# Loading a kernel's input into the upper half of its residual block, in one order with the weights

## The chip, the cores and the metric

The kernel runs on one core of one Trainium2 chip. The time is that of the device for one execution, in microseconds. An execution of a kernel on one core repeats to within 0.2%. A profile is one execution; its span is about 1.8 us shorter than the time.

Engines: PE is TensorE (matmuls, with PEld its weight loads), DVE is VectorE, ACT is ScalarE, POOL is GpSimd, SP is SyncE. L295 is line 295 of the kernel that the profile belongs to.

## The reference, cut to what matters

Four layers on x of 2048 x 1024 in bf16: linear attention (A), gated MLP (B), A, B, each with a layer norm in front and a residual add behind.

```python
def A(x, wqkv, wo):              # 32 heads of 32
    q, k, v = split(x @ wqkv)
    phi = lambda t: where(t > 0, t + 1, exp(t)) + 1e-6
    kv = einsum("bhsd,bhse->bhde", phi(k), v)
    z  = einsum("bhsd->bhd", phi(k))
    return (phi(q) @ kv / (phi(q) @ z + 1e-6)) @ wo
def B(x, Wg, Wu, Wd):
    g = x @ Wg
    return ((g * (g > 0)) * (x @ Wu)) @ Wd

x = x + A(layernorm(x));  x = x + B(layernorm(x))
x = x + A(layernorm(x));  x = x + B(layernorm(x))
```

## The kernel before

x is 16 row blocks of 128 rows, and a quarter is four blocks. For each quarter the attention layer normalises four blocks, transposes them into `xnT`, and runs 16 groups of eight 512-column matmuls: the two halves of the keys (k0, k1), then the two of the values (v0, v1), each for four blocks. Then come the small kv matmuls. When all four quarters are through, the query stage starts. The very first quarter is transposed by PE, all others by DMA transposes.

```python
def ln_norm(self, layer, t):
    src = self.xin.pop(t) if layer == 0 else self.x[t]      # xin: bf16 buffers, 3 of them
    ...bn_stats x2, bn_aggr (DVE); Ln, Exp (ACT) give rstd...
    nc.vector.tensor_scalar(out=xn, in0=src, ...)           # xn: 2 buffers
    if layer == 0:
        nc.gpsimd.tensor_copy(out=self.x[t], in_=src)       # bf16 -> fp32 residual
        if t + 3 < self.ST:
            self.load_x(t + 3)                              # issued on ACT's queue

def phi(self, ps, out):                                     # keys: ACT, then DVE twice
    nc.scalar.activation(out=e, in_=ps, func=ACT.Exp)
    nc.vector.tensor_scalar(out=e, in0=e, ...min, add)
    nc.vector.scalar_tensor_tensor(out=out, in0=ps, ..., in1=e)

# layer A, cut
ring.free_before((l, "k0"))                     # loads 7 weights of 1 MB on SP's queue
for q in range(self.NQ):
    if l == 0 and q == 0:
        for j in range(QT):
            self.ln_turn(l, j, self.ln_norm(l, j))          # PE transposes
    if q + 1 < self.NQ:
        self.ln_later(l, q + 1, 2, 4, 2)                    # norm + DMA transposes of the next quarter
    for c, name in enumerate(("k0", "k1", "v0", "v1")):
        for j in range(QT):
            ...eight matmuls into ps...
            ...keys: self.phi(ps, ...); values: one nc.scalar copy...
            if c == 3:
                later.at(2, lambda t=t: kv_step(t))
            later.tick()
```

## Time and profile before

| what | before |
|---|---|
| time, median of 4 runs | 1679.51 us (1679.11 to 1679.56) |
| first useful 512-column matmul | 14.82 us |
| first query matmul of layer 0 | 141.82 us |
| first gate matmul (layer 1) | 269.00 us |
| key/value stage of layer 2, which has no start-up | 117.58 us |

Read it from the end. PE is busy 98% of the span, so what counts is where PE is not busy or runs slowly. The waits of PE give the places, the timeline gives the moments, and a second pass over the same work (layer 2) gives the yardstick. The prediction below shows those lines.

### The profile page before, as it was taken

How to read it: one execution, taken by the hardware profiler on the slowest of the kernel's cores; microseconds unless marked ns; L12 is line 12 of the kernel's file. 1: busy time of each engine (PE TensorE's matmuls, PEld its weight loads, DVE VectorE, ACT ScalarE, POOL GpSimd, SP SyncE). 2: the span in 40 equal slices, each digit the busy share in tenths (PEclk: the TensorE clock that was granted, in tenths of full speed). 3: DMA queues.
4: the chain of work that ended last, by engine and by line, in shares of the span. 5: the costliest groups of instructions: out<-in, count | busy, mean ns of one | idle time of the engine just before them, and what ended most of it. 6: DMA issues, size and time to landing. Idle time of an engine off the chain costs nothing.

```text
span 1677.8 us, 18805 instructions
## 1 busy us (share of the span) xinstructions
PE 1651.6 (98%) x7824; PEld 752.0 (45%) x7824; DVE 572.4 (34%) x972; ACT 365.3 (22%) x693; POOL 20.9 (1%) x54
## 2 busy tenths in 40 slices
PE   6999999999999999999999999999999999999999
PEld 3444444444444444444444444444444444444444
DVE  6435895213211321321143289932111112211111
ACT  3335641110110111011023374411001101100110
POOL 2100000000000000000000000000000000000000
PEclk9999999999999999999999999999999999999999
DMA  9403133446545544654530222444554464465440
GB/s 270 82 25 121 31 82 94 148 154 184 166 136 163 158 152 158 183 157 136 168 99 1 76 76 38 95 120 141 170 186 152 131 192 136 146 188 165 147 152 28
DMA packets 261847, 218.28 MB, mean 130 GB/s; under 512 B 67201, under 2 KB 259713, under 8 KB 261761
## 3 DMA queue, kind: packets, MB, share of 16 engines
q1 hardware_dynamic: 254848, 208.69, 42.0%
q10 hardware_dynamic: 6912, 8.39, 1.6%
q8 instruction: 61, 1.00, 0.3%
q14 instruction: 26, 0.20, 0.0%
HBM read 197.13 MB, written 4.19 MB: 120 GB/s over the span
## 4 chain that ended last, share of the span: by engine, by line
PE 91%; DVE 5%; ACT 2%; DMA 2%; issue 1%; DVEq 0%; ACTq 0%
PE acc L383 23%; PE pu L366 23%; PE pg L366 23%; PE ps L232 12%; PE ps L301 5%; PE ps L314 3%; DVE stats L130 2%; DMA xin<-in_A_x_dram 1%; DVE xn L137 1%; PE kv L207 1%; PE ps L272 1%; DVE x L318 1%; DVE pq L276 0%; DMA xnT<-xn 0%; ACT r L274 0%
## 5 line engine op out<-in xcount | busy, mean ns | idle before, releaser
L366 PEld LDWEIGHTS <-t 128*128 128x128 bf16 x3584 | 350.7, 98 | 422.9
L366 PE MATMUL pg<-xnT,t 128*128 128x512 bf16 x1792 | 423.3, 379 | 0.0
L366 PE MATMUL pu<-xnT,t 128*128 128x512 bf16 x1792 | 423.3, 379 | 0.0
L383 PE MATMUL acc<-t,hT 128*128 128x512 bf16 x1792 | 388.1, 379 | 0.0
L372 DVE TENSOR_TENSOR hT<-pu,rg 128x512 bf16<-128x512 f32 x224 | 154.9, 692 | 591.5 <-PE pu L366 591.5
L371 ACT ACTIVATE rg<-pg 128x512 f32<-128x512 f32 x224 | 133.6, 597 | 764.9 <-PE pg L366 764.9
L383 PEld LDWEIGHTS <-hT 128*128 128x128 bf16 x1792 | 175.3, 98 | 211.4
L232 PE MATMUL ps<-t,xnT 128*128 128x512 bf16 x1024 | 229.1, 382 | 0.4 <-DVE pkv L179 0.4
L232 PEld LDWEIGHTS <-xnT 128*128 128x128 bf16 x1024 | 99.5, 98 | 115.5 <-issue 3.3
L301 PE MATMUL ps<-xnT,t 128*128 128x512 bf16 x512 | 121.3, 379 | 0.2
L314 PE MATMUL ps<-T,pq 128*128 128x512 bf16 x512 | 112.8, 379 | 0.0
L177 ACT ACTIVATE e<-ps 128x512 f32<-128x512 f32 x128 | 76.0, 594 | 82.0 <-PE ps L232 65.1
L178 DVE TENSOR_SCALAR e<-e 128x512 f32<-128x512 f32 x128 | 55.0, 430 | 112.0 <-ACT e L177 111.3
L134 ACT ACTIVATE rstd<-mv,eps 128x1 f32<-128x1 f32 x64 | 18.8, 295 | 321.0 <-DVE mv L132 320.8
L394 DVE TENSOR_TENSOR xo<-x,acc 128x512 bf16<-128x512 f32 x32 | 22.0, 688 | 171.1 <-PE acc L383 169.8
L314 PEld LDWEIGHTS <-pq 128*128 128x128 bf16 x512 | 50.1, 98 | 59.0
L301 PEld LDWEIGHTS <-t 128*128 128x128 bf16 x512 | 49.8, 98 | 55.5 <-issue 1.0
L391 DVE TENSOR_TENSOR x<-x,acc 128x512 f32<-128x512 f32 x32 | 21.6, 676 | 149.5 <-PE acc L383 148.4
L130 DVE BATCH_NORM_STATS2 stats<-x 128x6 f32<-128x512 f32 x96 | 66.2, 690 | 2.0
L238 ACT ACTIVATE pkv<-ps 128x512 bf16<-128x512 f32 x64 | 38.3, 598 | 75.2 <-PE ps L232 70.2
L276 DVE TENSOR_TENSOR pq<-pq,r 128x512 bf16<-128x512 bf16 x64 | 43.8, 689 | 7.9 <-ACT r L275 5.3
L274 ACT ACTIVATE r<-ps,eps 128x512 f32<-128x512 f32 x64 | 43.4, 686 | 9.0 <-PE ps L272 8.3
(41 smaller groups left out, 410.5 us busy)
## 6 DMA issues: line engine op xcount, KB each, us to landing
t<-in_B_W_gate_dram SPq DMA_DIRECT2D x56, 1024.0 KB, 6.0
t<-in_B_W_up_dram SPq DMA_DIRECT2D x56, 1024.0 KB, 5.3
t<-in_B_W_down_dram SPq DMA_DIRECT2D x64, 896.0 KB, 6.0
t<-in_A_wqkv_dram SPq DMA_DIRECT2D x12, 1024.0 KB, 6.6
xin<-in_A_x_dram ACTq DMA_DIRECT2D x16, 256.0 KB, 4.4
t<-in_A_wo_dram SPq DMA_DIRECT2D x4, 1024.0 KB, 5.2
out_dram<-xo ACTq DMA_DIRECT2D x32, 128.0 KB, 2.3
xnT<-xn SPq DMA_TRANSPOSE x60, 3.1
```

The lines of the kernel that those rows point to most:

```text
L130: nc.vector.bn_stats(out=stats[:, c, :], in_=src[:, c * fmax:(c + 1) * fmax])
L177: nc.scalar.activation(out=e, in_=ps, func=ACT.Exp)
L178: nc.vector.tensor_scalar(out=e, in0=e, scalar1=1.0, scalar2=1e-6, op0=ALU.min, op1=ALU.add)
L232: nc.tensor.matmul(ps, lhsT=self.xnT[l, q][:, kt, j * P:(j + 1) * P], rhs=w[:, kt, :], start=(kt == 0), stop=(kt == KT - 1))
L274: nc.scalar.activation(out=r, in_=ps, func=ACT.Ln, bias=self.eps6[:, 0:1])
L276: nc.vector.tensor_tensor(out=p, in0=p, in1=r, op=ALU.mult)
L301: nc.tensor.matmul(ps, lhsT=w[:, kt, (g % 4) * P:(g % 4 + 1) * P], rhs=self.xnT[l, sc][:, kt, :], start=(kt == 0), stop=(kt == KT - 1))
L314: nc.tensor.matmul(ps, lhsT=pq[sc, g // 4][:, g % 4, j * P:(j + 1) * P], rhs=T[g // 2][:, g % 2, n2 * NW:(n2 + 1) * NW], start=(g == 0), s ...
L366: nc.tensor.matmul(ps, lhsT=w[:, kt, fi * P:(fi + 1) * P], rhs=self.xnT[l, q][:, kt, :], start=(kt == 0), stop=(kt == KT - 1))
L371: nc.scalar.activation(out=rg, in_=pg, func=ACT.Relu)
L372: nc.vector.tensor_tensor(out=h[:, fi, :], in0=pu, in1=rg, op=ALU.mult)
L383: nc.tensor.matmul(acc[j], lhsT=hT[ft // 4][:, ft % 4, j * P:(j + 1) * P], rhs=wd[:, k, :], start=(ft == 0), stop=(ft == self.FT - 1))
```

## The change

The intent is to start PE sooner:

- x goes by DMA, as bf16, straight into the upper half of its own fp32 residual block. The cast on GpSimd and the three-buffer limit go away, and the residual add of layer 0 reads the bf16.
- All loads go out on SP's queue in one order: block 0 in halves, half of the first weight, block 1, and so on.
- Values ahead of keys, and the first eight groups in pairs of blocks, so that blocks 2 and 3 are wanted later.
- The transposes of each of the first four blocks in two halves; the identity made directly in bf16.
- Ten idle matmuls at the outset, for the clock.

```diff
+        self.xb = [x[:, D // 2:D].bitcast(BF16) for x in self.x]
-        src = self.xin.pop(t) if layer == 0 else self.x[t]
+        src = self.xb[t] if layer == 0 else self.x[t]
-        if layer == 0:
-            nc.gpsimd.tensor_copy(out=self.x[t], in_=src)
-            if t + 3 < self.ST:
-                self.load_x(t + 3)
-        self.nc.scalar.dma_start(out=xin, in_=self.x_v[:, t, :])
+        self.nc.sync.dma_start(out=self.xb[t][:, lo:hi], in_=self.x_v[:, t, lo:hi])
...
+    def head(self):
+        zero = self.ep.tile([P, NW], BF16, tag="e")
+        nc.vector.memset(zero, 0.0)
+        idle = self.ps3.tile([P, NW], F32, tag="b")
+        for _ in range(10):
+            nc.tensor.matmul(idle, lhsT=zero[:, 0:P], rhs=zero, start=True, stop=True)
+        self.load_x(0, 0)
+        self.load_x(0, 1)
+        ring.load_part(H)          # first half of v0
+        self.load_x(1)
+        ring.load_to(2)            # rest of v0, v1
+        self.load_x(2)
+        self.load_x(3)
+        ring.load_to(3)            # k0
+        ...blocks 4 to 7, k1, blocks 8 to 15, the other three weights...
...
-        for n in ("k0", "k1", "v0", "v1", "o0", "q0", "q1", "o1"):
+        for n in ("v0", "v1", "k0", "k1", "o0", "q0", "q1", "o1"):
...
+                order = [(c, j + i) for i in (0, 2) for c in range(2) for j in range(2)] + order[8:]
-                        later.at(2, lambda t=t: kv_step(t))
+                    later.at(3, lambda t=t: kv_step(t))
...
-        ident_f = self.xnp.tile([P, P], F32, tag="xn")
-        make_identity(nc, ident_f[:, :])
-        nc.vector.tensor_copy(out=self.ident, in_=ident_f)
+        make_identity(nc, self.ident[:, :])
```

More of the change, by code (lines that the diff above doesn't have):

```diff
@@ L23, in __init__, with load_part @@
         self.nc, self.pool, self.depth = nc, pool, depth
-        self.plan, self.tiles, self.loaded = [], {}, 0
+        self.plan, self.tiles, self.loaded, self.part = [], {}, 0, 0
     def add(self, name, src):
         self.plan.append((name, src))
+    def load_part(self, k):
+        name, src = self.plan[self.loaded]
+        t = self.pool.tile([P, 8, NW], BF16, tag="w")
+        self.nc.sync.dma_start(out=t[:, 0:k, :], in_=src[:, 0:k, :])
+        self.tiles[name], self.part = t, k
     def load_to(self, n):
@@ L31, in load_to @@
             name, src = self.plan[self.loaded]
-            t = self.pool.tile([P, 8, NW], BF16, tag="w")
-            self.nc.sync.dma_start(out=t[:, 0:src.shape[1], :], in_=src)
-            self.tiles[name] = t
+            if self.part == 0:
+                t = self.pool.tile([P, 8, NW], BF16, tag="w")
+                self.tiles[name] = t
+            k, m = self.part, src.shape[1]
+            self.nc.sync.dma_start(out=self.tiles[name][:, k:m, :], in_=src[:, k:m, :])
+            self.part = 0
             self.loaded += 1
@@ L93, in __init__ @@
         self.ep = pool("ep", 3)
-        self.xio = pool("xio", 3)
+        self.xo = pool("xo", 3)
         self.xnp = pool("xnp", 2)
@@ L102, in __init__ @@
         self.later = _Later()
-        self.n_evac = 0
-        ident_f = self.xnp.tile([P, P], F32, tag="xn")
         from concourse.masks import make_identity
-        make_identity(nc, ident_f[:, :])
         self.ident = self.const.tile([P, P], BF16, name="ident")
-        nc.vector.tensor_copy(out=self.ident, in_=ident_f)
+        make_identity(nc, self.ident[:, :])
         self.mask = self.const.tile([P, P], F32, name="mask")
@@ L118, in __init__, with ln_stat, ln_rstd @@
         self.x = [self.xres.tile([P, D], F32, name=f"x{t}") for t in range(self.ST)]
-        self.xin = {}
+        self.xb = [x[:, D // 2:D].bitcast(BF16) for x in self.x]
         self.xnT = {}
-    def ln_norm(self, layer, t):
-        nc, D = self.nc, self.D
-        src = self.xin.pop(t) if layer == 0 else self.x[t]
-        fmax = min(nc.vector.BN_STATS_FMAX, D)
-        nch = D // fmax
-        stats = self.small.tile([P, nch, nc.vector.BN_STATS_DIM], F32, tag="stats")
-        for c in range(nch):
-            nc.vector.bn_stats(out=stats[:, c, :], in_=src[:, c * fmax:(c + 1) * fmax])
+    def ln_stat(self, t, src, c, stats):
+        fmax = self.D // 2
+        self.nc.vector.bn_stats(out=stats[:, c, :], in_=src[:, c * fmax:(c + 1) * fmax])
+    def ln_rstd(self, stats):
+        nc = self.nc
         mv = self.small.tile([P, nc.vector.BN_AGGR_DIM], F32, tag="mv")
@@ L135, in ln_norm, with ln_scale @@
         nc.scalar.activation(out=rstd, in_=rstd, func=ACT.Exp, scale=-0.5)
-        xn = self.xnp.tile([P, D], BF16, tag="xn")
-        nc.vector.tensor_scalar(out=xn, in0=src, scalar1=mv[:, 0:1], scalar2=rstd[:, 0:1],
-                                op0=ALU.subtract, op1=ALU.mult)
-        if layer == 0:
-            nc.gpsimd.tensor_copy(out=self.x[t], in_=src)
-            if t + 3 < self.ST:
-                self.load_x(t + 3)
-        return xn
+        return mv, rstd
+    def ln_scale(self, src, mv, rstd, xn=None, h=None):
+        if xn is None:
+            xn = self.xnp.tile([P, self.D], BF16, tag="xn")
+        w = self.D // 2
+        s = slice(None) if h is None else slice(h * w, (h + 1) * w)
+        self.nc.vector.tensor_scalar(out=xn[:, s], in0=src[:, s], scalar1=mv[:, 0:1],
+                                     scalar2=rstd[:, 0:1], op0=ALU.subtract, op1=ALU.mult)
+        return xn
@@ new lines, in ln_norm, with turn @@
+    def ln_norm(self, layer, t):
+        nc = self.nc
+        src = self.xb[t] if layer == 0 else self.x[t]
+        stats = self.small.tile([P, 2, nc.vector.BN_STATS_DIM], F32, tag="stats")
+        for c in range(2):
+            self.ln_stat(t, src, c, stats)
+        xn = self.ln_scale(src, *self.ln_rstd(stats))
+        return xn
+    def head(self):
+        nc, tc, ring = self.nc, self.tc, self.ring
+        H = self.KT // 2
+        zero = self.ep.tile([P, NW], BF16, tag="e")
[11 more added lines that the diff above has]
+        ring.load_to(3)
+        self.load_x(4)
+        self.load_x(5)
+        self.load_x(6)
+        self.load_x(7)
+        ring.load_to(4)
+        for t in range(8, self.ST):
+            self.load_x(t)
+        ring.load_to(7)
+        src = self.xb
+        self.xnT[0, 0] = self.xnTp.tile([P, self.KT, QT * P], BF16, tag="xnT", name="xnT0_0")
+        stats = [self.small.tile([P, 2, nc.vector.BN_STATS_DIM], F32, tag="stats", name=f"st{j}")
+                 for j in range(QT)]
+        def turn(j, xn, h):
+            tp = self.ps3.tile([P, H, P], BF16, tag="b")
+            for i in range(H):
+                kt = h * H + i
+                nc.tensor.transpose(tp[:, i, :], xn[:, kt * P:(kt + 1) * P], self.ident)
+            dst = self.xnT[0, 0][:, h * H:(h + 1) * H, j * P:(j + 1) * P]
+            if h == 0:
+                nc.vector.tensor_copy(out=dst, in_=tp)
+            else:
+                nc.scalar.activation(out=dst, in_=tp, func=ACT.Copy)
+        with tc.manual_schedule(engines={mybir.EngineType.DVE, mybir.EngineType.Activation}):
+            for j in range(QT):
+                for c in range(2):
+                    self.ln_stat(j, src[j], c, stats[j])
+                r = self.ln_rstd(stats[j])
+                xn = self.xnp.tile([P, self.D], BF16, tag="xn")
+                for h in range(2):
+                    if j == 0 or h == 0:
+                        self.ln_scale(src[j], *r, xn, h if j == 0 else None)
+                    turn(j, xn, h)
@@ L150, in ln_turn @@
                                                 name=f"xnT{layer}_{q}")
-        dst = self.xnT[layer, q][:, :, j * P:(j + 1) * P]
-        if layer or q:
-            nc.sync.dma_start_transpose(out=dst, in_=xn)
-            return
-        tp = self.pst.tile([P, self.KT, P], BF16, tag="tr")
-        for kt in range(self.KT):
-            nc.tensor.transpose(tp[:, kt, :], xn[:, kt * P:(kt + 1) * P], self.ident)
-        self.n_evac += 1
-        if self.n_evac % 2:
-            nc.vector.tensor_copy(out=dst, in_=tp)
-        else:
-            nc.scalar.activation(out=dst, in_=tp, func=ACT.Copy)
+        nc.sync.dma_start_transpose(out=self.xnT[layer, q][:, :, j * P:(j + 1) * P], in_=xn)
     def ln_later(self, layer, q, first, step, lag):
@@ L180, in phi, with load_x @@
                                        op0=ALU.max, op1=ALU.add)
-    def load_x(self, t):
-        xin = self.xio.tile([P, self.D], BF16, tag="xio")
-        self.nc.scalar.dma_start(out=xin, in_=self.x_v[:, t, :])
-        self.xin[t] = xin
+    def load_x(self, t, c=None):
+        D = self.D
+        lo, hi = (0, D) if c is None else (c * D // 2, (c + 1) * D // 2)
+        self.nc.sync.dma_start(out=self.xb[t][:, lo:hi], in_=self.x_v[:, t, lo:hi])
     def plan_A(self, l):
@@ L200, in layer_A @@
         ring, later = self.ring, self.later
-        kv = [self.ps3.tile([P, NW], F32, tag="b", name=f"kv{l}_{i}") for i in range(3)]
         pk, va = {}, {}
@@ L212, in kv_step @@
             del pk[t], va[t]
-        ring.free_before((l, "k0"))
+        if l == 0:
+            self.head()
+        else:
+            ring.free_before((l, "v0"))
+        kv = [self.ps3.tile([P, NW], F32, tag="b", name=f"kv{l}_{i}") for i in range(3)]
         for q in range(self.NQ):
+            if q + 1 < self.NQ:
+                self.ln_later(l, q + 1, 4 if l == 0 and q == 0 else 2, 3 if l == 0 and q == 0 else 4, 2)
+            order = [(c, j) for c in range(4) for j in range(QT)]
             if l == 0 and q == 0:
-                for j in range(QT):
-                    self.ln_turn(l, j, self.ln_norm(l, j))
-            if q + 1 < self.NQ:
-                self.ln_later(l, q + 1, 2, 4, 2)
-            for c, name in enumerate(("k0", "k1", "v0", "v1")):
-                w = ring.get((l, name))
-                for j in range(QT):
-                    t = q * QT + j
-                    if c == 0:
-                        s = self.slab.tile([P, 2 * D + G], BF16, tag="slab", name=f"pkv{l}_{t}")
-                        pk[t] = s[:, 0:D]
-                        va[t] = s[:, D:2 * D + G].rearrange("p (g e) -> p g e", e=P + 1)
-                        nc.gpsimd.memset(va[t][:, :, P:P + 1], 1.0)
-                    ps = self.ps.tile([P, NW], F32, tag="a")
-                    for kt in range(KT):
-                        nc.tensor.matmul(ps, lhsT=self.xnT[l, q][:, kt, j * P:(j + 1) * P],
-                                         rhs=w[:, kt, :], start=(kt == 0), stop=(kt == KT - 1))
-                    if c < 2:
-                        self.phi(ps, pk[t][:, c * NW:(c + 1) * NW])
-                    else:
-                        g0 = (c - 2) * (NW // P)
-                        nc.scalar.activation(
-                            out=va[t][:, g0:g0 + NW // P, 0:P],
-                            in_=ps[:, :].rearrange("p (g e) -> p g e", e=P), func=ACT.Copy)
-                    if c == 3:
-                        later.at(2, lambda t=t: kv_step(t))
-                    later.tick()
@@ new lines, in layer_A @@
+                order = [(c, j + i) for i in (0, 2) for c in range(2) for j in range(2)] + order[8:]
+            for c, j in order:
+                w = ring.get((l, ("v0", "v1", "k0", "k1")[c]))
+                t = q * QT + j
+                if c == 0:
+                    s = self.slab.tile([P, 2 * D + G], BF16, tag="slab", name=f"pkv{l}_{t}")
+                    pk[t] = s[:, 0:D]
+                    va[t] = s[:, D:2 * D + G].rearrange("p (g e) -> p g e", e=P + 1)
+                    nc.gpsimd.memset(va[t][:, :, P:P + 1], 1.0)
+                ps = self.ps.tile([P, NW], F32, tag="a")
+                for kt in range(KT):
+                    nc.tensor.matmul(ps, lhsT=self.xnT[l, q][:, kt, j * P:(j + 1) * P],
+                                     rhs=w[:, kt, :], start=(kt == 0), stop=(kt == KT - 1))
+                if c >= 2:
+                    self.phi(ps, pk[t][:, (c - 2) * NW:(c - 1) * NW])
+                else:
+                    g0 = c * (NW // P)
+                    nc.scalar.activation(
+                        out=va[t][:, g0:g0 + NW // P, 0:P],
+                        in_=ps[:, :].rearrange("p (g e) -> p g e", e=P), func=ACT.Copy)
+                if c == 3:
+                    later.at(3, lambda t=t: kv_step(t))
+                later.tick()
@@ L316, in out_units @@
                                          start=(g == 0), stop=(g == G - 1))
-                    xs = self.x[t][:, n2 * NW:(n2 + 1) * NW]
-                    nc.vector.tensor_tensor(out=xs, in0=xs, in1=ps, op=ALU.add)
+                    cols = slice(n2 * NW, (n2 + 1) * NW)
+                    xs = self.x[t][:, cols]
+                    nc.vector.tensor_tensor(out=xs, in0=self.xb[t][:, cols] if l == 0 else xs,
+                                            in1=ps, op=ALU.add)
                     later.tick()
         ring.free_before((l, "o0"))
-        later.at(3, finish_kv)
-        q_units(0, 4)
+        later.at(4, finish_kv)
+        q_units(0, 5)
         fold_wo()
@@ L392, in layer_B @@
                         else:
-                            xo = self.xio.tile([P, NW], BF16, tag="xio")
+                            xo = self.xo.tile([P, NW], BF16, tag="xo")
                             nc.vector.tensor_tensor(out=xo, in0=xs, in1=acc[j], op=ALU.add)
@@ L402, in run @@
         nc.scalar.preload_act_table_set("natural_log_exp_and_others")
-        for t in range(3):
-            self.load_x(t)
         self.layer_A(0, 1)
```

## The prediction

> **What bounds the kernel now.** The page first: it says which engine sets the time.
>
> ```profile
> span 1677.8 us, 18805 instructions
> PE 1651.6 (98%) x7824; PEld 752.0 (45%) x7824; DVE 572.4 (34%) x972; ACT 365.3 (22%) x693; POOL 20.9 (1%) x54
> ```
>
> TensorE (PE) is busy for all but 26.2 us, so no change that leaves the matmuls alone can win more than that plus what cold-clock matmuls waste. Next, the waits of PE over the whole span (engine, tile, line, awaited instruction: total us, times, longest):
>
> ```profile
> PE tp L157 <- DVE ident L109: 12.2, 1, 12.2
> PE ps L272 <- DVE pq L179: 3.5, 6, 0.8
> PE tp L157 <- DVE xnT L160: 2.7, 2, 1.9
> PE kv L207 <- ACT pkv L238: 2.6, 1, 2.6
> ```
>
> Three of these four, 17.5 us, lie in the first 47 us of layer 0. The PE rows of the timeline there (start, us, line, operation, count, idle time before):
>
> ```profile
> 12.22 1.01 PE L157 MATMUL tp<-ident,xn 128*128 128x128 bf16 x8 [12.22 <-DVE ident L109]
> 14.02 1.01 PE L157 MATMUL tp<-ident,xn 128*128 128x128 bf16 x8 [0.78 <-DVE xnT L160]
> 14.82 2.76 PE L232 MATMUL ps<-t,xnT 128*128 128x512 bf16 x6
> 21.21 0.61 PE L157 MATMUL tp<-ident,xn 128*128 128x128 bf16 x8 [1.88 <-DVE xnT L160]
> 46.93 0.40 PE L207 MATMUL kv<-pkv 128*128 128x129 bf16 x4 [2.63 <-ACT pkv L238]
> ```
>
> The first useful 512-column matmul starts at 14.82, and six of them take 2.76 us (0.46 each). Layer 2 does the same work with no start-up, so I use it as the yardstick. Its key/value stage runs from 849.16 to 966.74 (first and last row below); layer 0's ends where line L301 takes over, at 141.82.
>
> ```profile
> 849.16 24.34 PE L232 MATMUL ps<-t,xnT 128*128 128x512 bf16 x112
> 966.74 1.89 PE L301 MATMUL ps<-xnT,t 128*128 128x512 bf16 x8
> 141.82 1.89 PE L301 MATMUL ps<-xnT,t 128*128 128x512 bf16 x8
> ```
>
> Layer 2: 117.58 us for 512 matmuls (0.216 us each, from 1.73 us per 8) plus the small kv ones. Layer 0: 141.82. **The whole start-up costs 24.2 us.** From L301 to the next layer both take about 127.2 us (layer 0's first gate matmul is at 269.00), so nothing else distinguishes them.
>
> Last, the chain of waits, for why layer 0 is late, and one row of the one-microsecond windows for the transfers (window, length, PE clock, DMA share, GB/s):
>
> ```profile
> 1.21 7.09 DMA xin<-in_A_x_dram
> 12.90 5.68 DMA xin<-in_A_x_dram
> 24.56 5.75 DMA xin<-in_A_x_dram
> 43.23 3.66 DMA xnT<-xn
> 13.00:14.00 1.00, 1.00 1.09 346
> ```
>
> Row blocks of x wait 5.7 to 7.1 us because three 1 MB weight loads run beside them and only three x buffers exist. The rate is about 250 GB/s from 2 to 4 us and 345 to 389 after: the transfers are saturated, so order decides. The identity's cast, a 0.20 us instruction queued late on DVE, holds the first transpose until 12.2.
>
> **What the Trainium skill says.** "TensorE: Matmul & The Clock Gate", Part 1: the array runs at half clock until busy for about 3.4 us, and falls back after an idle window of that length. The trace agrees: 0.46 us per matmul at 14.82 against 0.216 later, and 8 matmuls take 2.46 us on the chain after the 2.63 us gap at 43-47. "DMA: Bandwidth & Descriptors", section "Issuing engines are not separate DMA queues": issuing from two engines only saves issue time, the transfers interleave. The trace agrees: x loads (ACT queue) land 2.8 to 7.6 us after issue while the weights share the bandwidth. "SBUF — State Buffer", section "SBUF: two separate sides": DVE's two-port operations and GpSimd exclude each other. The trace agrees: normalising a block took 1.05 us beside a GpSimd cast, 0.55 us without.
>
> **The change part by part.** I use the built program's instruction order for the changed kernel and the durations above.
>
> 1. *One load order.* All of x and the seven weights (11.5 MB) go out on one queue. Estimated cumulative landing at 250 then 355 GB/s, plus 0.7 us to be seen: block 0 (two halves) about 3.3 us; half of v0, 5.5; block 1, 6.2; rest of v0, 7.7; v1, 10.7; block 2, 11.4; block 3, 12.1; k0, 15; k1, 21; the last weight about 36. Weights are in time: k0 is wanted near 23, k1 near 30.
>
> 2. *Path to the first matmul.* Two statistics at 0.65 (one already during the load), aggregation 0.19, the two small ScalarE steps 0.29 and 0.20, half a block normalised (about 0.3), with gaps: about 5.4. GpSimd now makes the identity in bf16 by about 2 us, so its wait (12.2) is gone.
>
> 3. *Idle matmuls.* Ten from 1.8 us, after the memset. At 0.43 cold and some warm at the end they finish near 5.9; they may hold the first transposes by half a microsecond, but the clock is then up, which saves about 1.5 us of cold matmuls. Four transposes, a copy: first useful matmul about 6.8 instead of 14.82.
>
> 4. *Pairs, values first.* After the eight matmuls of block 0, PE waits for block 1: its statistics start on DVE near 7.0 (1.3), aggregation, rstd, 0.55 of normalising: transposes at 9.7. Then 11 matmuls to 12.9. Block 2 lands at 11.4; the same DVE chain ends at 14.0, so PE idles about 1.1. Fifteen matmuls to 17.8, block 3 about 0.5 late: 18.3, its eight transposes end at 18.8. By then 34 matmuls (7.3 us) are done: **11.5 us lost** including 32 transposes. Values need only a ScalarE copy where keys need one ScalarE and two DVE steps (0.59, 0.43, 0.67), which leaves DVE to the statistics.
>
> 5. *Next quarter.* 94 matmuls and a kv step follow: the second quarter starts near 39.6. Its DMA transposes are queued behind all 11.5 MB, so the first lands near 38; an issue takes 1.23 us on SP, a landing 3.1 us or more, and only two normalised buffers exist, so the third lands near 42.3 and the fourth near 44. They are wanted at 44.5 and 46.2. DVE waits for these landings ahead of some key work, so a kv step may slip. I charge 0.8 us, against the 2.6 idle plus about 1.7 of cold clock after it today.
>
> 6. *No casts.* Sixteen GpSimd casts (1.04 each) and their wait for x are gone; GpSimd was never on PE's path, the gain is DVE's and already counted. The residual add reads bf16 instead of fp32; its 0.68 us is beside PE.
>
> Sum: loss in layer 0 falls from 24.2 to 11.5 + 0.8, about 12.3; the gain is 11.9. Layers 1 and 3 are unchanged. In layer 2 only the order of values and keys and the lag of kv change: no stall exists there to remove, and I count zero, within 1 us. 1679.5 - 11.9 = **1667.6 us**, 0.7% less.
>
> **Rivals.** *(a) The transpose wait replaces the x wait.* All 11.5 MB now stand ahead of the first DMA transpose. For it: the saturated rate, and the two-buffer chain. Against it: no x load competes with the transposes any more, and PE needs them only near 40. If the rate is 320 instead of 355, they come 3 to 4 us later, PE idles about 3 more and cools: about 1672. *(b) DVE sets the pace of the first four blocks*, not the loads: block 2 at the earliest near 13.3 in place of 14.0. For it: statistics, aggregation and normalising make some 3 us per block against 3.5 us of matmuls for its pair of value groups. The time would be 1666.5 to 1667, so nearly the same. *(c) The early gain is given back later*, because other waits absorb it. Against it: from 55 us on PE is full at the warm clock and the weights of the next stages are loaded ahead (the DMA share falls to 0.00 at 60-80 us), so an earlier start moves everything: no loss. *(d) The reordering hurts layers 0 and 2*: keys last put the long exp/min/max chain just before the kv steps and the end of the stage, where the masked kv is needed. Worth up to 1 or 2 us per layer: about 1670.
>
> **Range and chances.** Doubt is in the landing of block 2 (1 us), the transposes (-0.8 to +4) and the key order (-1 to +3): 1664.5 to 1672. Faster by 2% means below 1646; that is 33 us, more than all the start-up loss of 24.2. Slower by 2% would need 33 us of new stalls, and nothing here comes to that. So same: 0.98.
>
> **What would show it.** PE's first row: ten matmuls from about 1.8 us. First useful matmul at 6 to 8 us at about 0.22 to 0.25 us each; no wait on the identity. PE idle before the transposes of block 1 near 1 us, block 2 near 1, block 3 near 0.5. The first query-stage matmul of layer 0 near 130 instead of 141.8, and layer 2's stage still 117.6 long. Wrong if block 2's transposes start after 16 us, if PE idles over 3 us at 38-50, or if layer 2 gains new waits.

## The result, and the profile after

The changed kernel takes 1667.58 us, median of four runs (1667.28 to 1669.95), against 1679.51 (1679.11 to 1679.56). The ratio is 0.9933, with a 95% interval of 0.9915 to 0.995. That is the mean time of one kernel's runs over that of the other's of the same rounds, so not quite the ratio of the medians. The difference of the medians is 11.9 us, or 0.7%.

The page of the changed kernel:

```profile
span 1665.9 us, 18656 instructions
PE 1644.1 (99%) x7678; PEld 751.3 (45%) x7834; DVE 571.6 (34%) x975; ACT 364.9 (22%) x695; POOL 4.8 (0%) x38
```

The span is 11.9 us shorter. GpSimd's casts are gone (4.8 us busy instead of 20.9), and DVE and ScalarE do the same work as before. PE's sum can't be compared: its 7678 matmul records against 7834 weight loads show that about 150 are missing from this trace.

The waits of PE in the changed kernel over the whole span, without the query-stage ones (engine, tile, line, awaited instruction: total us, times, longest):

```profile
PE idle L171 <- DVE zero L168: 2.0, 1, 2.0
PE tp L198 <- DVE xn L149: 1.8, 2, 1.5
PE ps L295 <- DVE xnT L201: 0.8, 2, 0.5
PE ps L295 <- ACT xnT L203: 0.3, 1, 0.3
```

The wait of 12.2 us is gone, as are those of 2.7 and 2.6. Some 3 us remain in the first 20 us, apart from the two in front of the idle matmuls. PE's timeline of the changed kernel, cut:

```profile
1.95 4.45 PE L171 MATMUL idle<-zero 128*128 128x512 bf16 x10 [1.95 <-DVE zero L168]
...
7.34 0.61 PE L295 MATMUL ps<-t,xnT 128*128 128x512 bf16 x2 [0.52 <-DVE xnT L201]
...
10.25 0.62 PE L198 MATMUL tp<-ident,xn 128*128 128x128 bf16 x8 [0.34 <-DVE xn L149]
...
15.18 0.62 PE L198 MATMUL tp<-ident,xn 128*128 128x128 bf16 x8 [1.47 <-DVE xn L149]
...
19.13 0.62 PE L198 MATMUL tp<-ident,xn 128*128 128x128 bf16 x8
...
129.38 1.89 PE L364 MATMUL ps<-xnT,t 128*128 128x512 bf16 x8
...
257.13 1.89 PE L433 MATMUL pg<-xnT,t 128*128 128x512 bf16 x8
...
954.40 1.89 PE L364 MATMUL ps<-xnT,t 128*128 128x512 bf16 x8
```

The first useful matmul starts at 7.34 instead of 14.82; the rows at 10.25, 15.18 and 19.13 are the transposes of blocks 1, 2 and 3. The first gate matmul comes at 257.13 instead of 269.00, 11.87 us sooner, which is the whole difference. From there to the first matmul of layer 2 both kernels take 580.16 us. Layer 2's key/value stage, from 837.29 to 954.40, is 117.11 us long instead of 117.58. The 0.47 is one kv step (0.47 us) that has moved into the query stage; layer 2 as a whole takes 244.87 us against 244.74. So I read every experiment from the first gate matmul: what is not gained or lost by then is not gained or lost at all.

On the chain of waits (start, us, what), x now comes once in the start-up where it came three times before, and the DMA transpose that ended the chain's start at 43.23 is gone:

```profile
3.70 8.73 DMA x<-in_A_x_dram
```

That is the landing of block 2, issued at 3.7 and used at 12.45.

### The profile page after: what moved, and what is told of

The parts are those of the page before. It is cut to its first block, busy times and chain, and to the rows that moved or that the text cites. A ratio compares the mean times of both kernels' runs of the same rounds, so it can differ in the third digit from the quotient of the medians.

```text
span 1665.9 us, 18656 instructions
## 1 busy us (share of the span) xinstructions
PE 1644.1 (99%) x7678; PEld 751.3 (45%) x7834; DVE 571.6 (34%) x975; ACT 364.9 (22%) x695; POOL 4.8 (0%) x38
## 4 chain that ended last, share of the span: by engine, by line
PE 92%; DVE 4%; ACT 2%; issue 1%; DMA 1%; SPq 0%; another core or an unknown queue 0%
PE pg L433 23%; PE acc L450 23%; PE pu L433 23%; PE ps L295 13%; PE ps L364 4%; PE ps L377 4%; DVE stats L133 1%; PE kv L266 1%; DVE xn L149 1%; DVE x L384 1%; PE ps L335 1%; ACT r L337 1%; DMA x<-in_A_x_dram 1%; DVE pq L339 0%; ACT r L338 0%
## 5 line engine op out<-in xcount | busy, mean ns | idle before, releaser
L295 PE MATMUL ps<-t,xnT 128*128 128x512 bf16 x999 | 224.3, 379 | 2.3 <-DVE xnT L201 0.8
L133 DVE BATCH_NORM_STATS2 stats<-x 128x6 f32<-128x512 f32 (+1 forms) x120 | 81.5, 685 | 2.0
L149 DVE TENSOR_SCALAR xn<-x,mv,rstd 128x1024 bf16<-128x1024 f32 (+2 forms) x65 | 47.8, 737 | 25.5 <-DMA xnT<-xn 18.3
```

The costliest lines, as they stand in the source:

```text
L133: self.nc.vector.bn_stats(out=stats[:, c, :], in_=src[:, c * fmax:(c + 1) * fmax])
L149: self.nc.vector.tensor_scalar(out=xn[:, s], in0=src[:, s], scalar1=mv[:, 0:1], scalar2=rstd[:, 0:1], op0=ALU.subtract, op1=ALU.mult)
L295: nc.tensor.matmul(ps, lhsT=self.xnT[l, q][:, kt, j * P:(j + 1) * P], rhs=w[:, kt, :], start=(kt == 0), stop=(kt == KT - 1))
```

## The experiments

Twelve more runs were made, all correct; e12 is the changed kernel again. Times are medians; the last column is the first gate matmul of the profiled execution.

| run | what | time | runs from, to | gate |
|---|---|---|---|---|
| before | | 1679.51 | 1679.11, 1679.56 | 269.00 |
| changed | | 1667.58 | 1667.28, 1669.95 | 257.13 |
| e1 | before + bf16 identity | 1681.79 | 1681.5, 1682.08 | 271.49 |
| e2 | before + upper half, on ScalarE's queue | 1687.47 | 1687.22, 1687.65 | 277.01 |
| e3 | changed, one idle matmul | 1667.88 | 1667.61, 1668.3 | 257.74 |
| e4 | changed, blocks 2, 3 ahead of v1 | 1667.63 | 1667.14, 1667.85 | 256.58 |
| e5 | changed, keys first | 1670.24 | 1669.37, 1670.83 | 259.46 |
| e6 | changed, no pairs | 1672.84 | 1672.44, 1674.19 | 262.60 |
| e7 | changed, x on ScalarE's queue | 1683.75 | 1683.46, 1684.17 | 272.89 |
| e8 | changed, eight idle matmuls | 1668.03 | 1667.57, 1669.32 | 258.76 |
| e9 | e2 with x on SyncE's queue, in one order | 1669.76 | 1669.53, 1670.48 | 259.89 |
| e10 | changed, blocks 0 to 3 on ScalarE's queue | 1669.46 | 1669.27, 1669.69 | 258.74 |
| e11 | e4 + blocks 4 to 7 ahead of k0 | 1666.18 | 1665.88, 1666.23 | 255.62 |
| e12 | changed again, beside e11 | 1667.98 | 1667.39, 1668.8 | 257.05 |

In some executions the PE clock falls to half for 3.4 us, which costs up to 1.7 us. The profiled executions of before, e6, e8 and e10 contain one such stretch, that of e1 two, that of e7 a longer one; the others contain none before the gate. Each run's record has its mean PE clock, as a share of full speed.

### e1: the identity alone

```diff
-        ident_f = self.xnp.tile([P, P], F32, tag="xn")
-        make_identity(nc, ident_f[:, :])
-        nc.vector.tensor_copy(out=self.ident, in_=ident_f)
+        make_identity(nc, self.ident[:, :])
```

> The kernel before with one part of the change: the identity is made in bf16 by GpSimd, without the fp32 copy and the cast on DVE. The profile of before puts 12.2 us of PE's waiting down to that cast. Theory: the cast only stood last in a queue that waited for x anyway (block 0 normalised at 10.8, block 1 at 12.8, block 3 only after 20), so the gain is 0.5 to 1.5 us: about 1678.5. Rival, the wait is worth what it shows: the first transposes start near 2 to 6 us and 5 us or more are won, below 1674.5.

Measured: 2.3 us slower. PE's timeline of this run, its first and fourth transposes:

```profile
11.02 1.03 PE L155 MATMUL tp<-ident,xn 128*128 128x128 bf16 x8 [11.02 <-DVE xn L135]
...
22.31 0.62 PE L155 MATMUL tp<-ident,xn 128*128 128x128 bf16 x8 [1.59 <-DVE xn L135]
```

The wait of 12.2 us that the profile of before put down to the identity was in truth 11.0 us of waiting for x: take the identity away and the normalised block ends the wait, 1.2 us earlier. And the fourth transposes come later than before (22.31 against 21.21), because the order of DVE's instructions moved with the edit. The fourth row block's buffer is freed later, so the next load is issued at 22.33 instead of 20.63. Both theories missed: I had expected a small gain. What holds is that the identity was not worth its wait. Why the kernel is slower stays open. By the fourth transposes PE had done 17 matmuls instead of 12, so the 1.1 us are made up; the 2.5 us at the gate are a stretch at half clock from 23.1 to 26.5 us (1.7 us) and a longer wait before the kv matmuls (3.40 us against 2.63). But the three other runs, with a mean clock of 0.999 where the profiled one has 0.998, are only 0.1 to 0.6 us faster.

### e2: the upper half alone

```diff
-        xin = self.xio.tile([P, self.D], BF16, tag="xio")
-        self.nc.scalar.dma_start(out=xin, in_=self.x_v[:, t, :])
+        self.nc.scalar.dma_start(out=self.xb[t], in_=self.x_v[:, t, :])
-        for t in range(3):
+        for t in range(self.ST):
             self.load_x(t)
```

(with the cast removed and the residual add reading bf16, as in the change)

> The kernel before with only the loading into the upper half of the residual block: no cast, no three-buffer limit, all 16 loads issued at the start on ScalarE's queue, keys first, no pairs, no idle matmuls. Theory: the waits of 5.7 us for block 3 and the later ones for x vanish, about half of the change's gain: the key/value stage of layer 0 ends near 135 instead of 141.8, about 1673. Rival, the weights in front and the cold clock are what costs: less than 2 us won, over 1677.5.

Measured: 8.0 us slower than before, so both expectations were wrong. ScalarE's issues of transfers (ACTq) and PE's first transposes in this run:

```profile
0.76 21.12 ACTq L179 DMA_DIRECT2D x<-in_A_x_dram  x16
```

```profile
23.14 1.04 PE L153 MATMUL tp<-ident,xn 128*128 128x128 bf16 x8 [23.14 <-DVE xn L137]
```

Why is best seen in e7, which has the same fault in the changed kernel.

### e7: x on ScalarE's queue

```diff
-        self.nc.sync.dma_start(out=self.xb[t][:, lo:hi], ...)
+        self.nc.scalar.dma_start(out=self.xb[t][:, lo:hi], ...)
```

> The changed kernel with the loads of x on ScalarE's queue, as before, instead of in one order with the weights. Theory: the blocks then share the bandwidth with the weights, and loads that wait for an earlier landing hold up the small ScalarE steps of the normalisation behind them; the first useful matmul moves from 7.3 to 9 or later, 2 to 6 us lost: about 1671. Rival: all transfers run on the same 16 engines and the order hardly matters: within 0.7 us of 1667.6.

Measured: 1683.75 us, 16.2 us slower than the changed kernel and slower than the kernel before: the direction of the theory, which had 2 to 6 us. The timeline of ScalarE in this run (ACTq rows are issues of transfers):

```profile
0.76 20.06 ACTq L245 DMA_DIRECT2D x<-in_A_x_dram  x17
20.86 0.29 ACT L140 ACTIVATE rstd<-mv,eps 128x1 f32<-128x1 f32 x1 [18.86 <-DMA x<-in_A_x_dram]
```

Seventeen loads stand ahead of everything else in ScalarE's queue. In the built program the sixth issue and each one after it waits for an earlier landing, so the issuing drags on to 20.8 us. (In the packed traces of e2, e7, e10 and the changed kernel the loads of both queues share eight completion semaphores in turn: the first eight issues wait for nothing, the ninth waits until the first with its semaphore has landed.) The 0.29 us step that turns block 0's variance into a scale stands behind them; block 0's statistics were aggregated by 7.42. PE sits for 16.2 us. In the kernel before, each later load was issued one at a time, when a buffer came free; there a small step stood behind one issue at a time, as at 13.28, 0.66 us late.

### e10: only the first four blocks on ScalarE's queue

```diff
-        self.nc.sync.dma_start(out=self.xb[t][:, lo:hi], ...)
+        (self.nc.scalar if t < 4 else self.nc.sync).dma_start(out=self.xb[t][:, lo:hi], ...)
```

> The changed kernel with only row blocks 0 to 3 (five issues, none of which waits for a landing) on ScalarE's queue and all else as it is. Theory: what costs 16 us with all of x on that queue is that ScalarE's small steps stand behind issues that wait for landings; with five issues that wait for nothing, only the sharing of bandwidth with the weights is left: block 0 complete 1 to 3 us later, blocks 2 and 3 perhaps earlier, the query stage of layer 0 within 1.5 us of 129.4: 1666.5 to 1669. Rival: the sharing itself is the cost, 1675 or more.

Measured: 1669.46 us, the gate at 258.74: 1.5 to 1.9 us slower than the changed kernel (1667.58 and, beside it, 1667.98). That is a little over the upper end stated, 1669, and far from the rival's 1675. With five issues that wait for nothing, ScalarE is not held up: its first small step runs at 7.32, as soon as the statistics are aggregated. PE's timeline, the transposes of the first half of block 0 and of block 1:

```profile
8.35 0.40 PE L198 MATMUL tp<-ident,xn 128*128 128x128 bf16 x4 [1.95 <-DVE xn L149]
...
12.47 1.06 PE L198 MATMUL tp<-ident,xn 128*128 128x128 bf16 x8
```

The first transposes start at 8.35 instead of 6.19, because the weights take their part of the bandwidth while block 0 comes in. After this idle start the PE clock is at half from 10.3 to 13.7 us (the eight transposes take 1.06 us instead of 0.62), which is worth up to 1.7 us of work; all four runs have a mean clock of 0.999. So sharing the bandwidth for these four blocks costs 1.5 to 1.9 us, and much of it may come through the clock. Of the 16.2 us of e7, 13.4 pass while ScalarE's first small step stands behind issues (7.42 to 20.86). What sharing alone costs when all sixteen blocks are on that queue was not run.

### e9: upper half and one order, nothing else

```diff
 # e2, and:
-        self.nc.scalar.dma_start(out=self.xb[t], in_=self.x_v[:, t, :])
+        self.nc.sync.dma_start(out=self.xb[t], in_=self.x_v[:, t, :])
+            # layer 0: block 0, k0, block 1, k1, blocks 2 and 3, v0, blocks 4 to 7, v1, the rest
```

> The kernel of the second experiment (upper half, keys first, no pairs, no idle matmuls, fp32 identity with its cast) with the loads of x moved from ScalarE's queue to SyncE's, in the changed kernel's order among the weights. Theory: there, ScalarE stood behind 16 load issues until 21.9 us, and that was the whole loss; without it the first transposes start near 7 us instead of 23.1, and the query stage of layer 0 begins near 135, so about 1673, 14 us less than the second experiment. Rival: the upper half or the fp32 identity is slow by itself, above 1680.

Measured: 1669.76 us, 17.7 us less than e2 and 9.7 less than before. The mechanism was as expected, and the gain was larger. PE's timeline of this run, its first transposes and first useful matmuls:

```profile
9.34 1.01 PE L153 MATMUL tp<-ident,xn 128*128 128x128 bf16 x8 [9.34 <-DVE ident L109]
...
12.00 4.40 PE L239 MATMUL ps<-t,xnT 128*128 128x512 bf16 x11
```

Here the late cast of the identity does cost something: block 0 was normalised at 6.1 us, and PE waits for the cast until 9.3. The first useful matmuls are at half clock, 0.40 us each. Still, this kernel without pairs, without values first, without halves, without idle matmuls and with the old identity has 9.7 of the 11.9 us. **Loading x into its place, in one order, from an engine with nothing else to do, is most of the change.** e9 changes the queue and the order together; e7 and e10 are what tells them apart. No run has the loads in one order into separate bf16 buffers, so what the place inside the residual block is worth is not shown.

### e5 and e6: keys first, no pairs

```diff
 # e5
-        for n in ("v0", "v1", "k0", "k1", "o0", ...):
+        for n in ("k0", "k1", "v0", "v1", "o0", ...):
 # e6
-                order = [(c, j + i) for i in (0, 2) for c in range(2) for j in range(2)] + order[8:]
+                order = [(c, j + i) for i in (0,) for c in range(2) for j in range(4)] + order[8:]
```

> The changed kernel with keys ahead of values again, pairs kept. Theory: each key group needs 1.1 us of DVE that the statistics and normalising of the next blocks want, so the transposes of blocks 2 and 3 and the DMA transposes of the next quarter come later and PE loses 1 to 3 us: about 1669.5. Rival: the landing of block 2 at 12.4 us sets the pace and DVE has room: within 0.4 us of 1667.6.

> The changed kernel with the first groups in the order of the row blocks (first value half for all four, then the second) instead of in pairs. Theory: when the transposes of block 3 end, 24 matmuls are done instead of 34, and these 10 matmuls of 0.216 us are lost: 2.2 us, about 1669.8. Rival: the transposes themselves come earlier since PE is free, and less than 0.5 us is lost.

Measured: 1670.24 us and 1672.84 us, 2.7 and 5.3 slower than the changed kernel. For e5 the size was as expected but not the place. Up to the first kv step it is level with the changed kernel (38.07 against 38.15). The loss comes in the second quarter, in PE's and DVE's timelines of e5:

```profile
53.87 1.89 PE L295 MATMUL ps<-t,xnT 128*128 128x512 bf16 x7 [1.66 <-DVE pkv L239]
```

```profile
52.21 0.55 DVE L149 TENSOR_SCALAR xn<-x,mv,rstd 128x1024 bf16<-128x1024 bf16 x1 [0.68 <-DMA xnT<-xn]
```

DVE normalises the blocks to come, and each of these steps waits for a DMA transpose to give back one of two buffers. With keys first, key work (L239) stands in the same queue behind such a step, and PE runs out of result buffers and waits 1.66 us. With values first, that quarter's key work on DVE begins at 58.14, after the last of those waits.

For e6, PE's timeline, the transposes of blocks 2 and 3:

```profile
15.79 0.62 PE L198 MATMUL tp<-ident,xn 128*128 128x128 bf16 x8 [2.73 <-DVE xn L149]
...
20.20 0.62 PE L198 MATMUL tp<-ident,xn 128*128 128x128 bf16 x8 [1.59 <-DVE xn L149]
```

PE idles longer (2.73 and 1.59 us instead of 1.47 and none). By the transposes of block 3, 1.1 us later than in the changed kernel, it has done 24 matmuls instead of 34; these ten are the 2.2 us that I expected. It then waits another 0.4 us for their copy. The surprise is the clock: its mean from 20 to 25 us is 0.66, where the changed kernel has 1.00. Windows of half a microsecond show 0.50 from 21.3 to 24.8: 3.4 us at half clock, or 1.7 us of work lost. The four make 5.4, against 5.5 at the gate.

Note that e9 has neither pairs nor values first and is faster than e6. The parts do not add up; each is worth something only against the waits that the others leave.

### e3 and e8: the idle matmuls

```diff
-        for _ in range(10):
+        for _ in range(1):     # e3; 8 in e8
```

> The changed kernel with one idle matmul instead of ten. Theory: the first matmuls run at half clock; eight of block 0 take 3.5 us instead of 1.7 (0.5 us of it beyond the wait for block 1), and the next eleven may be cold in part, so 1 to 3 us are lost: about 1669.5. Rival, PE waits for the row blocks anyway and the cold matmuls fill that wait: within 0.4 us of the changed kernel's 1667.6.

> The changed kernel with eight idle matmuls instead of ten. In its profile the ten end at 6.2 us, cold throughout, while block 0 was normalised at 5.5: they hold the first transposes by 0.6 us. Theory: the first useful matmul moves from 7.3 to about 6.9 but block 2 lands at 12.4 as before, so nothing is won: within 0.3 us of 1667.6. Rival: the whole start moves by 0.4 us, 1667.1; or the clock now comes up later and 1 us or more is lost.

Measured: 1667.88 and 1668.03 us, the same as the changed kernel within the spread of its own runs (1667.58, and 1667.98 in e12). For e3 the rival holds. PE's timeline of e3:

```profile
9.38 1.44 PE L295 MATMUL ps<-t,xnT 128*128 128x512 bf16 x3 [0.45 <-DMA t<-in_A_wqkv_dram]
...
15.79 0.62 PE L198 MATMUL tp<-ident,xn 128*128 128x128 bf16 x8 [1.47 <-DVE xn L149]
```

The matmuls are cold (0.48 us each at 9.38; the clock column reads 1.00 there, but it does so too while the ten idle matmuls take 0.44 us each, so in the first microseconds I go by durations), but PE has to wait for the second half of the weight until 9.4 and for block 2 until 15.8 anyway. The cold matmuls fill time in which it would have stood idle. So the idle matmuls are worth about 0.3 us by the medians, 0.6 by the profiles, not the 1.5 I had written.

In e8 the first useful matmul starts at 6.48 instead of 7.34 and nothing is won, as expected: PE waits 1.30 us for the weight's second half and 2.06 for block 2. The profiled execution is 1.6 us late at the gate all the same. From its windows (window, length, busy time and count of PE, PEld, DVE, ACT and POOL, PE clock, DMA share, GB/s) and its PE timeline:

```profile
15.00:20.00 5.00, 4.37 (x19) 2.36 (x21) 3.57 (x8) 1.84 (x5) 0.00 (x0) 0.66 1.07 367
```

```profile
15.41 1.03 PE L198 MATMUL tp<-ident,xn 128*128 128x128 bf16 x8 [2.06 <-DVE xn L149]
```

The gap of 2.06 us was followed by about 3.4 us at half clock: the eight transposes take 1.03 us instead of 0.62. It does not happen in every execution: the mean clock is 0.999 in two runs of e8 (1669.32 and 1668.45) and 1.0 in the two others (1667.61 and 1667.57). The changed kernel's own slower runs (1669.95 in the first set, 1668.8 twice in e12) have 0.999 as well and its other six 1.0; 3.4 us at half clock in 1666 us are 0.999. So they are most likely the same fallback, though no trace was taken of them.

### e4, e11 and e12: what is left

```diff
 # e4                                   # e11 as well
-        ring.load_to(2)
+        ring.load_to(1)
         self.load_x(2)
         self.load_x(3)
-        ring.load_to(3)
+        ring.load_to(3)                # e11: ring.load_to(2), and k0 with k1 after blocks 4 to 7
```

> The changed kernel with row blocks 2 and 3 loaded ahead of the second value weight instead of after it. Theory: the landing of block 2 sets the start of its transposes at 15.2 us; 1 MB earlier they start at 13.9, where the DVE chain allows, and about 1.3 us are won: 1666.3, if the second value weight, now landing near 12.7, is still in time for its first use near 12.9. Rival: PE then waits for that weight instead and nothing is won, 1667.6 or more.

> The changed kernel with row blocks 2 and 3 ahead of the second value weight (as in the fourth experiment) and blocks 4 to 7 ahead of the first key weight. In the fourth experiment DVE, before it could aggregate block 3, waited 0.98 us for block 4, whose statistics stand ahead in its queue. Theory: that wait goes, the transposes of block 3 start near 17.7 instead of 18.6, the query stage of layer 0 near 128.0 instead of 129.4: about 1666.2, ahead of the changed kernel by 1.4. Rival: the gain of the fourth experiment (0.55 us in its profile) is all there is: 1667.1 or more.

> The changed kernel itself, timed beside the eleventh on the same chip. Expected: 1667.6 again, the query stage of layer 0 at 129.4 in the profile, some executions about 2 us longer where the clock falls back in the first 20 us. If the time lies within 0.4 us of the eleventh's, that one is no improvement.

In the changed kernel block 2's statistics start when it lands, at 12.45. With e4 they start at 10.82 and PE's transposes of block 2 at 13.56 instead of 15.18, with no wait. But the time is 1667.63, no gain that the timing could show, and 0.55 us at the gate. The theory named the right wait and missed the next. From DVE's timeline in e4, then PE's:

```profile
16.58 0.69 DVE L133 BATCH_NORM_STATS2 stats<-x 128x6 f32<-128x512 bf16 x1 [0.98 <-DMA x<-in_A_x_dram]
```

```profile
18.59 0.62 PE L198 MATMUL tp<-ident,xn 128*128 128x128 bf16 x8 [1.18 <-DVE xn L149]
```

In DVE's order the statistics of block 4 stand ahead of the aggregation of block 3. Block 4 comes after the first key weight, so block 3, long landed, waits for block 4. e11 moves blocks 4 to 7 ahead of that weight as well:

```profile
13.69 0.62 PE L198 MATMUL tp<-ident,xn 128*128 128x128 bf16 x8
...
17.64 0.62 PE L198 MATMUL tp<-ident,xn 128*128 128x128 bf16 x8
```

Neither of the two rows of e11 shows a wait. The gate comes at 255.62 and the time is 1666.18 us (expected: 1666.2). Beside it on the same chip the changed kernel takes 1667.98; the runs of the two (1665.88 to 1666.23, and 1667.39 to 1668.8) do not overlap. e11 beats both kernels, the one before by 13.3 us.

## Why the prediction was right

The prediction said 1667.6 us and 1667.58 was measured. The agreement to 0.02 us is luck, since terms of the sum were off in both directions. The frame held.

- **The yardstick.** The start-up cost 24.2 us against layer 2, and nothing after it would move. It held: 580.16 us from the gate to layer 2 in both kernels. *Rival (c)*, the gain given back later, is out.
- **Path to the first matmul.** Said 6.8, measured 7.34. The ten idle matmuls ran cold throughout (4.45 us) and held the first transposes to 6.19, although the first half of block 0 was normalised at 5.5.
- **Pairs, values first.** Said transposes at 9.7, 14.0 and 18.3 and 34 matmuls done by 18.8; measured 10.25, 15.18 and 19.13, and the next matmul at 19.59. That is 0.8 us more lost. The largest single miss was the landing of block 2: said 11.4, its statistics started at 12.45.
- **Next quarter.** Charged 0.8 us; measured nothing. From 19.59 to 129.38 are 109.79 us, and 478 matmuls at 0.216 with 14 kv steps at 0.47 make 109.8. The DMA transposes were in time: the two normalised buffers were written again at 38.33, against my estimate of near 38. *Rival (a)* is out, and these two misses cancel.
- **Rivals (b) and (d).** (b) took DVE as the pace in place of the landing of block 2, for 0.6 to 1.1 us less time. The landing was the pace, as I had it; with e4 it is gone and DVE's order shows next. (d), that the reordering would hurt, is out: keys first costs 2.7 us, and layer 2 is the same to 0.13 us.
- **What was mis-sized.** The warm clock: "saves about 1.5 us of cold matmuls", in fact 0.3. I counted a saving on PE where PE waits anyway. I also read the slow matmuls after the 2.63 us gap as agreeing with an idle window of 3.4 us; the gap is shorter, so they do not (see the last section). The identity: I wrote "its wait (12.2) is gone" as a step of the path. It is one only after x comes early: alone it gave nothing (e1), and with one load order it was worth up to the 3 us that PE waits for it in e9.
- **Where the gain comes from.** The prediction spread it over the parts without weighing them. The runs do: upper half and one order on SyncE give 9.7 us of 11.9 (e9), and the other parts together give the rest, though each of two, undone alone, costs more than that.
- **What I did not see.** I cited the Trainium skill's "DMA: Bandwidth & Descriptors", section "Issuing engines are not separate DMA queues", that a second issuing engine only saves issue time, and gave the choice of the issuing engine no term of its own in the sum. e7 shows that it matters more than any part that I did count: 16.2 us, for an engine that has other work behind issues that wait.

## What to carry to other kernels

When a start-up is slow, find a later pass over the same work and take the difference as the ceiling. Then order all first loads on one engine that does nothing else, in the order in which the consumers' queues will ask for them, including blocks whose statistics merely stand ahead in a queue. A wait in the profile names the last to arrive: before an edit is built on it, ask what would have ended the wait a moment earlier.

## What the Trainium skill lacked or had wrong

- "DMA: Bandwidth & Descriptors", section "Issuing engines are not separate DMA queues": it says that issuing on several engines saves only issue time. The section lacks that an issue can wait for an earlier landing and hold the engine's own instructions (the page says elsewhere only that such a wait is the issuing sequencer's), and no page says what that costs: ScalarE's first small step ran at 20.86 us behind 17 issues, and the kernel lost 16.2 us (e7). With five issues that wait for nothing it lost 1.5 to 1.9 (e10).
- "TensorE: Matmul & The Clock Gate", Part 1: it gives an idle window of about 3.4 us as what brings the half clock back. (A later passage of Part 1 reports falls from frequent short idle times, without a figure.) Here no window had to be idle. The clock fell after a gap of 2.06 us in e8, and in the kernel before 1.2 us after a gap of 2.63 us had ended. In the first 55 us of these traces it fell from full to half seven times, and PE had worked in the 3.4 us before each fall: 1.23 us (before), 1.16 and 0.90 (e1), 1.44 (e6), 0.86 (e7), 1.35 (e8) and 1.40 (e10). With the traces cut every 3.4 us from the moment of the first clock change, the stretches there that kept the full clock have 1.61 us of work or more. The length of the cold phase agrees with the page: 3.4 us each time, and 17 us in e7, where PE stood still. The ten idle matmuls took 4.45 us, all at half clock, but 3.74 us in e7, so the moment of warming varies, as the page says.
- No page says that warming matmuls are worth nothing where the first matmuls wait for data in any case: nine of ten taken away changed the time by 0.3 us (e3).
